# A routed expert layer: six experts in the order of their row counts, with graded capacities and shorter halves

## The chip, the cores and the metric

The kernel runs on one core of a Trainium2 chip. The metric is the device time of one execution in microseconds (us). Its engines work beside each other: TensorE (PE) multiplies matrices, with a separate row for its weight loads (PEld); VectorE (DVE) and ScalarE (ACT) work on elements; GpSimd (POOL) does elementwise work too and issues the indirect transfers; SyncE (SP) issues the plain transfers (DMA).

## The reference

The last of three stages is the one that changes. Before it, attention runs with 16 clusters over 2 batches of 768 tokens, 8 heads of 64, and then a dense feed-forward layer with 2048 hidden columns. Its output, 1536 tokens of 512 numbers, goes into a layer with eight experts; each token is computed by two of them:

```python
def _moe2_ref(x, w_gate, w_noise, noise, w1, w2):
    N, D = x.shape
    E = w_gate.shape[1]
    logits = x @ w_gate
    noise_scale = np.log1p(np.exp(x @ w_noise))
    noisy_logits = logits + noise_scale * noise
    top2 = np.argpartition(-noisy_logits, 2, axis=1)[:, :2]
    ...
    for e in range(E):
        for k in range(2):
            mask = top2[:, k] == e
            ...
            h = np.maximum(x[mask] @ w1[e], 0.0)
            out[mask] += top2_w[mask, k, None] * (h @ w2[e])
```

N is 1536, D is 512, E is 8, and `w1[e]` is 512 x 1024. So 3072 rows are computed in all, and how many an expert gets is known only once the gate has run on the chip.

## The kernel before, in words

All large matmuls are done in a split float form: each operand is kept as a high part and a remainder, and one product takes three matmuls (high by high, high by remainder, remainder by high).

The gate's result gives each token and each of its two experts a slot. `route_scatter` writes the token's row of 516 numbers (512 values and 4 of weights and indices) into a DRAM tensor `xs`, in which each expert has a region of its own; POOL issues one indirect transfer for 128 rows (L965). `route_end` (L972 to 977) then knows how many rows each expert has, and `table` (L979 to 995) writes a small table to DRAM (`tab`, L987) and computes `nr`, the number of passes over the experts. One pass is enough where no expert overflows its capacity; `rest` (L1343 on) loops over further passes and needs `nr` in a register of each engine (L1345).

Each expert is computed for a fixed number of rows, its capacity; slots behind the last real row are computed and thrown away. Experts 0 and 1 have 512 slots in two halves of HALF = 256 rows, one per batch. Their first halves (batch 0) are begun inside `middle`, beside the end of the dense layer, by a list of due times. Their second halves come in `moe2` (L1310 to 1341): `gather_half` (L1055 to 1060) fetches `Xh`, 128 partitions of 2 rows, once the scatters have landed. Experts 2 to 7 follow in the order of their numbers, each with CAP = 432 rows, 108 partitions by 4 (L1334 to 1341).

For each of these `load` fetches weights and rows. `weights` (L1040 to 1046) issues eight transfers of 512 KB in a fixed order into three staging buffers (`stg`, L1008 and L1010); ACT makes the high part (L1017) and DVE or POOL the remainder (L1021). This runs about one expert ahead of its use. `gather` (L1048 to 1052) fetches the rows `X` from the expert's region of `xs` into the one buffer "R". `turn` transposes `X` on TensorE (L1121), in tiles of 128 by 108, into `xT`, which ACT and DVE split (L1123, L1124), and computes the tokens' weights and indices from the last four columns (L1070 to 1075). After `turn` the buffer "R" is free for the next gather.

`expert` (L1275 to 1308) is the work proper. The first layer (L1217) keeps a piece of the weights stationary and moves all rows of `xT` as columns, 432 at a time: 8 blocks of hidden columns by 4 blocks of inputs by 3, 96 matmuls. ACT makes the relu (L1225), DVE the remainder (L1226). The second layer has two forms. For experts 2 to 6 (`flip`, `ffn2_t`, L1270) the rows are again the moving columns, 8 by 4 by 3 = 96 matmuls of 432 columns, and the result is transposed back (L1308). For the last expert and for the halves (`ffn2`, L1240) a block of rows is stationary and 512 columns of weights move: one set of 24 matmuls per block, four blocks of 108 rows for the last expert. `combine` scales each block by the token's weight (L1252, or L1254 where it is added to what another expert left) and POOL writes it to the output by an indirect transfer (L1255); `gather_out` (L1100, L1102) fetches beforehand what is there.

The order in which an engine gets its instructions comes from the program's order and a scheduler that ranks ready work; in `middle`, and on TensorE at the end of the last expert, it is written by hand.

Of the kernel before, what the change touches and what calls it, by code (L numbers as in the profile page):

```python
# [8 lines left out]
F32 = mybir.dt.float32  # L9
F32R = mybir.dt.float32r  # L10
# [11 lines left out]
NB = S // 128  # L22
# [5 lines left out]
E = 8  # L28
# [4 lines left out]
CK = CAP // CP  # L33
HALF = 256
MAIN = 2 * HALF
BASE = MAIN - CAP
ROUNDS = -(-NT // CAP)
REG = BASE + ROUNDS * CAP
ROW = DM + 4
# [562 lines left out]
class Moe:  # L602
# [39 lines left out]
    def init_piece(self, i):  # L642
        nc = self.nc
        n = E * CK
        if i < n:
            e, k = divmod(i, CK)
            cp = CP if e > 1 else 128
# [324 lines left out]
    def route_end(self):  # L972
        v, end = self.nc.vector, self.rtot[:, NB, 0:2]
        over = self.rtile("over", 2)
        v.tensor_scalar(over, end, float(-MAIN), 0.0, op0=OP.add, op1=OP.max)
        v.scalar_tensor_tensor(end, over, float(MAIN), self.over[:, 0], op0=OP.add, op1=OP.add)
        self.table(self.rtot[:, NB, :])

    def table(self, total):  # L979
# [3 lines left out]
        for r in range(ROUNDS):  # L983
            v.tensor_scalar_add(tb[:, r, :, 0], total, float(-BASE - r * CAP))
            v.tensor_scalar(tb[:, r, :, 1], self.ie, float(REG), float(BASE + r * CAP), op0=OP.mult, op1=OP.add)
            v.tensor_copy(tb[:, r, :, 2], self.ie)
        nc.sync.dma_start(self.tab.rearrange("(o r) n -> o (r n)", o=1), tb[0:1].rearrange("p r e n -> p (r e n)"))  # L987
        mx = self.const.tile([128, 1 + ROUNDS], F32, name="mx")
        v.tensor_reduce(mx[:, 0:1], total, axis=AX.X, op=OP.max)
        v.memset(mx[:, 1:2], 1.0)  # L990
        for r in range(1, ROUNDS):
            v.tensor_single_scalar(mx[:, r + 1:r + 2], mx[:, 0:1], float(BASE + r * CAP), op=OP.is_gt)
        self.nr = self.const.tile([128, 1], I32, name="nr")
# [45 lines left out]

    def weights(self, e, par=None):  # L1040
        fixed = par is None
        we = [w[e] if fixed else w[bass.ds(e, 1)].rearrange("o k n -> (o k) n") for w in (self.w1, self.w2)]
        W = [None] * 8
        for s in ORDER:
            W[s] = self.weights_part(e, e % 2 if fixed else par, s, we)
        return [x for p in W for x in p]

    def gather(self, e):  # L1048
        X = self.rows.tile([CP, CK, ROW], F32, tag="R", name="X")
        o = e * REG + BASE  # L1050
        self.nc.sync.dma_start(X, self.xs[o:o + CAP].rearrange("(p k) n -> p k n", k=CK))
        return X

    def gather_half(self, b):

        X = (self.rows if b else self.yp).tile([128, 2, 2, ROW], F32, tag="R" if b else "Y", name="Xh")
        for e in range(2):
# [20 lines left out]
    def gather_rest(self, e, r):  # L1078
# [6 lines left out]
                       allow_small_or_imprecise_dtypes=True)  # L1085
        v.tensor_scalar(sl[:, :, 1:2], sl[:, :, 0:1], t[:, 0:1], OOB, op0=OP.is_lt, op1=OP.mult)
        v.scalar_tensor_tensor(ix, sl[:, :, 0:1], t[:, 1:2], sl[:, :, 1:2], op0=OP.add, op1=OP.add)
# [4 lines left out]
        X = self.rows.tile([CP, CK, ROW], F32, tag="R", name="X")  # L1092
        nc.sync.dma_start(X, self.xs[bass.ds(e * REG + r * CAP + BASE, CAP)].rearrange("(p k) n -> p k n", k=CK))
        return X, self.meta(X[:, :, DM:], t[:, 2:3])
# [16 lines left out]

    def xtile(self):
        return self.xg.tile([128, KB, 2, CAP], F32R, tag="xT", name="xT")

# [11 lines left out]
    def middle(self, acc, W0, xT0, m0, we):  # L1126
# [53 lines left out]
        for fb in range(FB2):  # L1180
# [3 lines left out]
            def g(fb=fb):  # L1184
                if fb == 0:
                    ps.extend(self.bank((k,), [128, DM]) for k in (5, 6))
                self.ffn2(W0, ps, t["H", fb], fb)
# [125 lines left out]
    def moe2(self, W0, W1, xT1, m1):  # L1313
# [6 lines left out]

        self.expert(W1, xT1, m1, True, 128, second)
        self.expert(W0, nxt[0][1], nxt[0][2], False, 128, lambda: self.xpose(*nxt[1][:2], (6, 7)))

        def load(e):
            n["W"] = self.weights(e)
            n["X"] = self.gather(e)

        def turn(e):
            n["xT"] = self.xtile()
            self.xpose(n["X"], n["xT"], (6, 7))  # L1330
            n["m"] = self.meta(n["X"][:, :, DM:], float(e))

        load(2)
        done = lambda: None  # L1334
        self.expert(W1, nxt[1][1], nxt[1][2], True, 128, lambda: turn(2))
# [125 lines left out]
```

## Time and profile before

| | us |
|---|---|
| median of 3 runs | 966.37 |
| lowest, highest | 964.11, 972.53 |
| the profiled execution | 959.64 |
| its span, first to last instruction | 957.9 |

The profiled execution is 6.7 us below the median of the three runs; durations are taken from it. A busy time is an engine's own work and leaves out waits. A timeline row groups instructions that follow each other: its first number is the start of the first of them in us, its second the time to the modelled end of the last; ends of matmuls overlap the next one's start, so prices of matmuls are taken from start to start. The mean granted TensorE clock was 0.977 of 2.4 GHz.

### The profile page before, as it was taken

What the parts mean: (1) busy time and instruction counts of PE and PEld (TensorE: products, weight loads), DVE (VectorE), ACT (ScalarE), POOL (GpSimd) and SP (SyncE); (2) the same over time, 40 slices, a digit from 0 to 9 for tenths busy, and PEclk for the clock granted to TensorE, in tenths of its full rate; (3) what the DMA queues carried; (4) which work ended last, traced back from release to release, by engine and by line L of the source; (5) the groups of instructions that cost most, each with busy time, mean ns of one, the idle gap of its engine ahead of it and who ended that gap; (6) DMA issues with size and microseconds to landing.
All of it is one profiled execution on the core that took longest, in us unless ns stands there. A gap on an engine that the chain in (4) does not pass through costs nothing. (4 is left out here: it accounts for less than half of the span.)

```text
span 957.9 us, 14851 instructions
## 1 busy us (share of the span) xinstructions
PE 901.3 (94%) x5305; PEld 818.6 (85%) x5305; DVE 603.1 (63%) x1175; ACT 493.6 (52%) x1021; POOL 360.5 (38%) x400
## 2 busy tenths in 40 slices
PE   6999999999895999999999999999999999999993
PEld 3898989898784988889998989889899999999982
DVE  3889998999875677775447554826555554543321
ACT  2788888888875556554445434415434343341210
POOL 3134443445528777660000501552342433323121
PEclk8899999999998999999999998999999999999997
DMA  8756675676304433402010420464764555542011
GB/s 210 188 146 181 161 206 142 174 199 182 118 19 138 128 104 121 132 11 72 30 44 23 163 81 23 132 232 163 247 178 154 150 171 152 169 124 68 27 43 36
DMA packets 77680, 120.73 MB, mean 126 GB/s; under 512 B 9777, under 2 KB 55858, under 8 KB 76954
## 3 DMA queue, kind: packets, MB, share of 16 engines
q1 hardware_dynamic: 70114, 101.57, 36.8%
q0 software_dynamic: 7488, 18.16, 5.9%
q8 instruction: 43, 0.70, 0.3%
q14 instruction: 35, 0.29, 0.1%
HBM read 73.70 MB, written 24.36 MB: 102 GB/s over the span
## 5 line engine op out<-in xcount | busy, mean ns | idle before, releaser
L422 DVE TENSOR_TENSOR PTl<-ps_pt,PTh 128x384 fp32r<-128x384 f32 x192 | 98.4, 548 | 10.1 <-ACT PTh L417 9.2
L417 ACT ACTIVATE PTh<-ps_pt 128x384 fp32r<-128x384 f32 x192 | 87.5, 495 | 28.0 <-PE ps_pt L407 26.7
L390 DVE TENSOR_REDUCE nm<-ps_s 128x1 f32<-128x768 f32 x96 | 91.1, 948 | 12.6 <-PE ps_s L385 12.1
L729 PE MATMUL bank<-xh,wih 128*128 128x384 f32 x256 | 88.3, 345 | 10.0 <-ACT wih L713 5.0
L729 PE MATMUL bank<-xh,wil 128*128 128x384 f32 x256 | 88.3, 345 | 6.3 <-POOL wil L714 6.3
L407 PE MATMUL ps_pt<-ident,P 128*128 128x128 f32 x576 | 88.0, 276 | 4.0 <-DVE PTl L422 3.5
L398 ACT ACTIVATE P<-ps_s,nm 128x768 f32<-128x768 f32 x96 | 87.4, 910 | 5.3 <-DVE nm L390 5.3
L1217 PE MATMUL bank<-xT,wB 128*128 128x432 f32 (+1 forms) x480 | 87.1, 329 | 0.0
L729 PE MATMUL bank<-xl,wih 128*128 128x384 f32 x256 | 87.0, 340 | 0.0
L1225 ACT ACTIVATE hh<-bank 128x432 fp32r<-128x432 f32 (+1 forms) x80 | 36.8, 464 | 95.7 <-PE bank L1217 89.7
L1217 PEld LDWEIGHTS bank<-xT,wB 128*128 128x128 f32 x480 | 78.4, 188 | 4.2
L407 PEld LDWEIGHTS ps_pt<-ident,P 128*128 128x128 f32 x576 | 67.8, 141 | 15.1 <-DVE PTl L422 11.9
L1226 DVE SCALAR_TENSOR_TENSOR hl<-bank,hh 128x432 fp32r<-128x432 f32 (+1 forms) x80 | 42.0, 528 | 59.5 <-ACT hh L1225 59.2
L744 PE MATMUL bank<-woh,gh 128*128 128x512 f32 x192 | 76.2, 397 | 0.6 <-DVE Xn L484 0.6
L1021 POOL TENSOR_TENSOR wA<-stg,wA 128x512 fp32r<-128x512 f32 x16 | 20.7, 1292 | 146.8 <-DVE wol L714 69.7
L744 PE MATMUL bank<-wol,gh 128*128 128x512 f32 x192 | 75.4, 393 | 0.0
L744 PE MATMUL bank<-woh,gl 128*128 128x512 f32 x192 | 71.5, 394 | 0.0
L384 PE MATMUL ps_s<-k,q 128*128 128x384 f32 x192 | 70.2, 366 | 0.2 <-ACT P L398 0.2
L385 PE MATMUL ps_s<-k,q 80*128 80x384 f32 x192 | 66.4, 346 | 3.9 <-DMA q<-ohT 3.9
L1255 POOL DMA_INDIRECT out_dram<-Y,idx x32 | 35.7, 1117 | 74.3 <-DVE Y L1254 66.5
L729 PEld LDWEIGHTS bank<-xh,wih 128*128 128x128 f32 x256 | 49.0, 191 | 12.7 <-ACT wih L713 5.4
L1017 ACT ACTIVATE wA<-stg 128x512 fp32r<-128x512 f32 x52 | 32.4, 632 | 49.4 <-DMA stg<-in_moe_w_dram 22.4
(280 smaller groups left out, 2251.1 us busy)
## 6 DMA issues: line engine op xcount, KB each, us to landing
stg<-in_moe_w_dram SPq DMA_DIRECT2D x64, 512.0 KB
q<-ABq SPq DMA_DIRECT2D x48, 192.0 KB
k<-ABk SPq DMA_DIRECT2D x48, 192.0 KB
si<-in_moe_w_in_dram SPq DMA_DIRECT2D x14, 512.0 KB
so<-in_moe_w_out_dram SPq DMA_DIRECT2D x14, 512.0 KB
xs<-zrow SPq DMA_DIRECT2D x24, 217.7 KB
X<-xs SPq DMA_DIRECT2D x6, 870.8 KB
ld<-in_k_dram SPq DMA_DIRECT2D x8, 384.0 KB
```

Of the source, the lines that this page charges most:

```text
L384: self.nc.tensor.matmul(o, self.g("S1", u, "q")[:, h, qs], self.g("S1", u, "k")[:, h, ks], start=True, stop=False)
L385: self.nc.tensor.matmul(o, self.g("S2", u, "q")[:80, h, qs], self.g("S2", u, "k")[:80, h, ks], start=False, stop=True)
L390: self.nc.vector.tensor_reduce(nm, self.g("s", j)[:, :, :384], axis=AX.XY, op=OP.max, negate=True)
L398: self.nc.scalar.activation(P, self.t.pop(("s", j))[:, :, :384], AF.Exp, bias=self.t.pop(("nm", j)), scale=1.0, accum_out=self.g("sums", u ...
L407: self.nc.tensor.transpose(ps[:, k, :], P[:, k * 128:(k + 1) * 128], self.ident)
L417: self.nc.scalar.activation(self.pt_at(j, g, 0), self.g("pt", j, g), AF.Copy)
L422: self.nc.vector.tensor_sub(self.pt_at(j, g, 1), self.t.pop(("pt", j, g)), f(self.pt_at(j, g, 0)))
L729: nc.tensor.matmul(h, w[:, kb, :], x[b][:, kb, sl], start=(kb == 0 and x is self.xh and w is wih), stop=(kb == KB - 1 and w is wil))
L744: nc.tensor.matmul(acc[j], g[:, sl], w, start=(fb == 0 and n == 0), stop=(fb == FB1 - 1 and n == 2))
L1217: self.nc.tensor.matmul(ps, w[:, kb, :], xT[:, kb, x], start=(kb == 0 and i == 0), stop=(kb == KB - 1 and i == 2))
L1225: self.nc.scalar.activation(hh, ps, AF.Relu)
L1226: self.nc.vector.scalar_tensor_tensor(hl, ps, 0.0, f(hh), op0=OP.max, op1=OP.subtract)
```

## The change

- HALF falls from 256 to 240, held as 120 partitions by 2 rows.
- Experts 2 to 7 run in the order of their row counts, largest first. The place in that order sets the capacity: 432, 416, 408, 400, 392 and 384. The last place is three blocks of 128 rows, the others four blocks of 108, 104, 102, 100 and 98.
- The order is found on DVE in a new function `rank` between `route_end` and `table`. SP reads each place's expert number into a register, and the addresses of the weights and of `X` are computed from it. `turn` compares with the expert number out of a tile.
- `table` and the overflow passes take account of the graded capacities, with three rounds in place of four.

```diff
-HALF = 256
+HALF = 240
+CH = HALF // 2
...
+CAPS = ((108, 4), (104, 4), (102, 4), (100, 4), (98, 4), (128, 3))
+CMIN = min(cp * ck for cp, ck in CAPS)
...
+        self.rank(self.rtot[:, NB, :])
         self.table(self.rtot[:, NB, :])
+    def rank(self, total):
+        c, v, n = self.const, self.nc.vector, E - 2
...
+        v.scalar_tensor_tensor(key, total[:, 2:], float(E), self.ie[:, 2:], op0=OP.mult, op1=OP.subtract)
...
+        v.tensor_tensor(big, row(key), col(key), op=OP.is_gt)
+        v.tensor_reduce(pos.rearrange("p (n o) -> p n o", o=1), big, axis=AX.X, op=OP.add)
+        v.tensor_tensor(big, row(pos), col(self.ie[:, :n]), op=OP.is_equal)
...
+        v.tensor_copy(self.ordi, self.ord)
...
-    def weights(self, e, par=None):
-        fixed = par is None
-        we = [w[e] if fixed else w[bass.ds(e, 1)].rearrange("o k n -> (o k) n") for w in (self.w1, self.w2)]
+    def weights(self, e, par):
+        we = [w[bass.ds(e, 1)].rearrange("o k n -> (o k) n") for w in (self.w1, self.w2)]
...
-    def gather(self, e):
-        X = self.rows.tile([CP, CK, ROW], F32, tag="R", name="X")
-        o = e * REG + BASE
-        self.nc.sync.dma_start(X, self.xs[o:o + CAP].rearrange("(p k) n -> p k n", k=CK))
+    def gather(self, e, cp, ck):
+        X = self.rows.tile([cp, ck, ROW], F32, tag="R", name="X")
+        self.nc.sync.dma_start(X, self.xs[bass.ds(e * REG + BASE, cp * ck)].rearrange("(p k) n -> p k n", k=ck))
...
         def load(e):
-            n["W"] = self.weights(e)
-            n["X"] = self.gather(e)
+            i = self.nc.values_load(self.ordi[0:1, e - 2:e - 1], engines=(mybir.EngineType.SP,), min_val=2, max_val=E - 1)
+            n["W"] = self.weights(i, e % 2)
+            n["X"] = self.gather(i, *CAPS[e - 2])
...
         def turn(e):
-            n["xT"] = self.xtile()
+            cp, ck = CAPS[e - 2]
+            n["xT"] = self.xtile(cp * ck)
...
-            done = self.expert(W, xT, m, True, CP, lambda: turn(e + 1) if e + 1 < E else None, done, e == E - 1,
+            done = self.expert(W, xT, m, True, CAPS[e - 2][0], lambda: turn(e + 1) if e + 1 < E else None, done, e == E - 1,
                                e < E - 1)
```

TensorE gets 24 matmuls fewer in all, those of the fourth block of the last expert. Instructions that wait for a register, and what the scheduler ranks behind them, stand elsewhere on SP and on TensorE. First SP, while the first halves end: the first weight load of the first of the six experts (`stg_8029` before), the table, and what goes before the gather `X`. Before:

```order
L1008 DMA stg_8029<-in_moe_w_dram 128x4x256
L987 DMA tab<-tb 1x128
L1345 TENSOR_LOAD nr
L1345 ISA x2
L1010 DMA stg_8037<-in_moe_w_dram 128x2x512
L1008 DMA stg_8047<-in_moe_w_dram 128x4x256
L1059 DMA Xh<-xs 128x1032 x2
L1010 DMA stg_8055<-in_moe_w_dram 128x2x512
L1008 DMA stg_8065<-in_moe_w_dram 128x4x256
L1051 DMA X<-xs 108x2064
```

With the change, the same place up to the table (`stg_8064` is the first weight load of the first of the six):

```order
L1045 DMA stg_7590<-in_moe_w_dram 128x2x512
L1359 TENSOR_LOAD ordi
L1359 ISA x2
L1043 ISA
L1043 DMA stg_8064<-in_moe_w_dram 128x4x256
L1359 TENSOR_LOAD ordi
L1359 ISA x2
L1019 DMA tab<-tb 1x128
L1359 TENSOR_LOAD ordi
```

The first weight load now stands behind a register load of `ordi`, the order, and four more register loads follow the rows shown before `nr` is read. Further down on SP the gather `X` came behind five of that expert's weight loads before (the last row of the first piece); now it comes behind all eight:

```order
L1043 DMA stg_8100<-in_moe_w_dram 128x4x256
L1045 ISA
L1045 DMA stg_8110<-in_moe_w_dram 128x2x512
L1043 ISA
L1043 DMA stg_8120<-in_moe_w_dram 128x4x256
L1045 ISA
L1045 DMA stg_8130<-in_moe_w_dram 128x2x512
L1084 ISA
L1084 DMA X<-xs 108x2064
L1043 ISA
```

What moved there is the gather: the three weight loads that followed it now go ahead of it. Last, TensorE, where the transposes of `X` for the first of the six experts begin. `xT_7763` and `xT_7797` are the transposed rows of experts 0's and 1's second halves in the two programs, `hh` a relu result. Before, they begin in the second half of expert 0:

```order
L1217 MATMUL bank_7948<-xT_7763,wA_6296 128x256
L1121 MATMUL bank_8297<-ident,X 128x108 x4
L1121 MATMUL bank_8304<-ident,X 128x108
L1240 MATMUL bank_7814<-wA_6872,hh_7938 128x512
L1240 MATMUL bank_7814<-wA_6873,hh_7938 128x512
L1240 MATMUL bank_7815<-wA_6872,hh_7938 128x512
L1240 MATMUL bank_7815<-wA_6873,hh_7938 128x512
L1121 MATMUL bank_8304<-ident,X 128x108 x2
L1217 MATMUL bank_7965<-xT_7763,wA_6299 128x256 x2
L1217 MATMUL bank_7965<-xT_7763,wA_6300 128x256
L1217 MATMUL bank_7965<-xT_7763,wA_6299 128x256 x2
```

With the change:

```order
L1251 MATMUL bank_8161<-xT_7797,wB_7185 128x240
L1251 MATMUL bank_8161<-xT_7797,wB_7184 128x240 x2
L1251 MATMUL bank_8161<-xT_7797,wB_7185 128x240
L1155 MATMUL bank_8332<-ident,X 128x108 x4
L1155 MATMUL bank_8339<-ident,X 128x108
L1251 MATMUL bank_8192<-xT_7797,wB_7358 128x240 x2
L1251 MATMUL bank_8192<-xT_7797,wB_7359 128x240
L1251 MATMUL bank_8192<-xT_7797,wB_7358 128x240 x2
L1251 MATMUL bank_8192<-xT_7797,wB_7359 128x240
L1251 MATMUL bank_8192<-xT_7797,wB_7358 128x240 x2
L1251 MATMUL bank_8192<-xT_7797,wB_7359 128x240
L1274 MATMUL bank_8142<-wB_7207,hh_8157 120x512
```

The transposes moved from the second half of expert 0 into that of expert 1, behind the second group of its first layer's matmuls; the matmuls around them are 240 columns wide in place of 256.

## Rows read from the trace of the kernel before

**Rows 1.** The page: busy us (share of the span) and instructions of TensorE.
```profile
PE 901.3 (94%) x5305; PEld 818.6 (85%) x5305; DVE 603.1 (63%) x1175; ACT 493.6 (52%) x1021; POOL 360.5 (38%) x400
```

**Rows 2.** Windows: us; busy of PE, PEld, DVE, ACT, POOL (instructions); PEclk; DMA share; GB/s.
```profile
734.60:775.43 40.83, 40.83 (x224) 38.86 (x223) 22.36 (x36) 14.73 (x30) 15.63 (x12) 1.00 0.49 152
775.43:816.43 41.00, 41.00 (x225) 38.99 (x224) 22.51 (x40) 16.99 (x33) 14.50 (x12) 1.00 0.57 167
816.43:857.76 41.33, 41.32 (x225) 39.04 (x224) 20.20 (x37) 14.79 (x29) 14.22 (x12) 1.00 0.47 144
857.76:898.86 41.10, 41.10 (x226) 38.96 (x225) 14.69 (x27) 8.86 (x18) 9.63 (x9) 1.00 0.21 62
898.86:941.70 42.84, 42.84 (x209) 35.83 (x207) 12.58 (x18) 4.46 (x9) 11.19 (x11) 1.00 0.16 49
941.70:957.90 16.20, 0.15 (x1) 0.00 (x0) 0.75 (x1) 0.00 (x0) 1.12 (x2) 0.57 0.09 27
```

**Rows 3.** Waits of TensorE from 580 to 693 us: total, times, longest.
```profile
PE bank L1121 <- DMA Xh<-xs: 1.3, 1, 1.3
```

**Rows 4.** Timeline of TensorE: start us, us, line, tiles, shapes, count.
```profile
576.18 0.34 PE L729 MATMUL bank<-xh,wih 128*128 128x384 f32 x1
...
578.27 0.38 PE L1121 MATMUL bank<-ident,Xh 128*128 128x128 f32 x2
...
650.77 1.58 PE L1217 MATMUL bank<-xT,wg 128*128 128x256 f32 x12
652.19 1.09 PE L1240 MATMUL bank<-wA,hh 128*128 128x512 f32 x4
653.12 0.62 PE L1240 MATMUL bank<-wA,hl 128*128 128x512 f32 x2
...
788.98 2.53 PE L1217 MATMUL bank<-xT,wA 128*128 128x432 f32 x12
791.35 0.56 PE L1270 MATMUL bank<-hh,wA 128*128 128x432 f32 x2
...
814.88 0.91 PE L1121 MATMUL bank<-ident,X 108*128 108x108 f32 x8
815.56 0.45 PE L1270 MATMUL bank<-hl,wA 128*128 128x432 f32 x1
```

**Rows 5.** Waits of SP's queue from 605 to 700 us.
```profile
SPq L1059 <- DMA xs<-R,rridx: 6.1, 2, 5.6
```

**Rows 6.** Timeline of SP, 605 to 700 us: weight loads and gathers.
```profile
618.06 0.37 SPq L1008 DMA_DIRECT2D stg<-in_moe_w_dram  x1
...
630.95 0.39 SPq L1010 DMA_DIRECT2D stg<-in_moe_w_dram  x1
...
638.94 0.83 SPq L1059 DMA_DIRECT2D Xh<-xs  x2
...
655.64 1.49 SPq L1051 DMA_DIRECT2D X<-xs  x1
...
663.20 0.37 SPq L1010 DMA_DIRECT2D stg<-in_moe_w_dram  x1
...
682.11 0.33 SPq L1051 DMA_DIRECT2D X<-xs  x1
...
689.23 0.37 SPq L1010 DMA_DIRECT2D stg<-in_moe_w_dram  x1
```

**Rows 7.** Timeline of DVE, where the row counts are done.
```profile
619.15 0.16 DVE L976 SCALAR_TENSOR_TENSOR rtot<-rover,over 128x2 f32<-128x2 f32 x1
```

**Rows 8.** Line L1345, register load of nr on SP: ns min/median/max.
```profile
L1345 SPq TENSOR_LOAD <-nr x1: 702/702/702, 621.9 to 621.9; - x1
```

**Rows 9.** Timeline of TensorE, transposes of X for experts 2 and 3.
```profile
663.74 0.65 PE L1121 MATMUL bank<-ident,X 108*128 108x108 f32 x5
...
672.98 0.54 PE L1121 MATMUL bank<-ident,X 108*128 108x108 f32 x4
...
688.36 0.66 PE L1121 MATMUL bank<-ident,X 108*128 108x108 f32 x5 [0.35 <-DMA X<-xs]
```

More of the change, by code (lines that the diff above doesn't have):

```diff
@@ L982, in table @@
         v.memset(tb, 0.0)
-        for r in range(ROUNDS):
-            v.tensor_scalar_add(tb[:, r, :, 0], total, float(-BASE - r * CAP))
-            v.tensor_scalar(tb[:, r, :, 1], self.ie, float(REG), float(BASE + r * CAP), op0=OP.mult, op1=OP.add)
+        for r in range(1, ROUNDS):
+            o = BASE + CMIN + (r - 1) * CAP
+            v.tensor_scalar_add(tb[:, r, :, 0], total, float(-o))
+            v.tensor_scalar(tb[:, r, :, 1], self.ie, float(REG), float(o), op0=OP.mult, op1=OP.add)
             v.tensor_copy(tb[:, r, :, 2], self.ie)
+        v.tensor_scalar_add(tb[:, 1, :, 3], self.cap, float(-CMIN))
         nc.sync.dma_start(self.tab.rearrange("(o r) n -> o (r n)", o=1), tb[0:1].rearrange("p r e n -> p (r e n)"))
         mx = self.const.tile([128, 1 + ROUNDS], F32, name="mx")
-        v.tensor_reduce(mx[:, 0:1], total, axis=AX.X, op=OP.max)
+        left = self.const.tile([128, E], F32, name="left")
+        v.scalar_tensor_tensor(left, self.cap, float(BASE), total, op0=OP.add, op1=OP.is_lt)
+        v.tensor_mul(left, left, total)
+        v.tensor_reduce(mx[:, 0:1], left, axis=AX.X, op=OP.max)
         v.memset(mx[:, 1:2], 1.0)
         for r in range(1, ROUNDS):
-            v.tensor_single_scalar(mx[:, r + 1:r + 2], mx[:, 0:1], float(BASE + r * CAP), op=OP.is_gt)
+            v.tensor_single_scalar(mx[:, r + 1:r + 2], mx[:, 0:1], float(BASE + CMIN + (r - 1) * CAP), op=OP.is_gt)
         self.nr = self.const.tile([128, 1], I32, name="nr")
@@ L1110, in xpose, with xtile @@
             self.xpose_part(X, xT, kb, banks)
[L1112 to L1113 removed]
+    def xtile(self, n=CAP):
+        return self.xg.tile([128, KB, 2, n], F32R, tag="xT", name="xT")
     def xpose_part(self, X, xT, kb, banks):
@@ L1185, in g @@
                 if fb == 0:
-                    ps.extend(self.bank((k,), [128, DM]) for k in (5, 6))
+                    ps.extend(self.bank((k,), [CH, DM]) for k in (5, 6))
                 self.ffn2(W0, ps, t["H", fb], fb)
@@ L1319, in second @@
             self.xpose(*nxt[0][:2], (6, 7))
[L1321 to L1322 removed]
+        self.expert(W1, xT1, m1, True, CH, second)
+        self.expert(W0, nxt[0][1], nxt[0][2], False, CH, lambda: self.xpose(*nxt[1][:2], (6, 7)))
         def load(e):
[L1325 to L1326 removed]
+            i = self.nc.values_load(self.ordi[0:1, e - 2:e - 1], engines=(mybir.EngineType.SP,), min_val=2, max_val=E - 1)
+            n["W"] = self.weights(i, e % 2)
+            n["X"] = self.gather(i, *CAPS[e - 2])
         def turn(e):
[L1329 removed]
+            cp, ck = CAPS[e - 2]
+            n["xT"] = self.xtile(cp * ck)
             self.xpose(n["X"], n["xT"], (6, 7))
[L1331 removed]
+            n["m"] = self.meta(n["X"][:, :, DM:], self.ord[:cp, e - 2:e - 1])
         load(2)
         done = lambda: None
[L1335 removed]
+        self.expert(W1, nxt[1][1], nxt[1][2], True, CH, lambda: turn(2))
         for e in range(2, E):
```

31 lines of the change are left out of this document (24 added, 7 removed).

## The prediction

> **What bounds the kernel now.** I read the page first: TensorE is busy for 94% of the span and no other engine comes near [rows 1], so the first guess is that only matmul time counts. A share over the whole span proves nothing about one stage, so the second view is the table of windows, cut at the last layer's experts. From expert 3 on every window is TensorE from end to end: 40.83 of 40.83 us, 41.00 of 41.00, 41.32 of 41.33, 41.10 of 41.10, and 42.84 of 42.84 for expert 7, at granted clock 1.00 (2.4 GHz), with DVE at most 22.5 us and the DMA engines at most 0.57 busy [rows 2]. So there a column less is time less, until DVE or the weights become the limit, and they have 18 us of room in each expert. Behind the last matmul lies a tail of 16.20 us that holds no expert work [rows 2]; the change doesn't touch it. Third, the waits of TensorE over the halves of experts 0 and 1: it stands 1.3 us for `Xh`, the second halves' rows [rows 3]. There a shorter matmul turns into a longer wait; the gathers of `X` for experts 2 and 3 come close to it too (below). Fourth, the price of a matmul. Durations of single matmuls overlap in the profile, so I take start to start in the timeline: 256 columns (652.19 − 650.77)/12 = 0.118 us, 384 columns, twelve of them before the next kind, (578.27 − 576.18)/12 = 0.174, 432 columns (791.35 − 788.98)/12 = 0.1975, 512 columns (653.12 − 652.19)/4 = 0.2325 [rows 4]. From 256 to 432 that is 0.45 ns a column; from 432 to 512 it is 0.44, from 384 to 432 it is 0.49. I take 0.45 and keep 0.44 and 0.49 as ends.
>
> **The change part by part.**
>
> Capacities of experts 3 to 6. Each of these runs 96 first-layer matmuls (8 blocks, 4 x 3) and 96 second-layer ones with the rows as moving columns, 192 together. The second to fifth place lose 16, 24, 32 and 40 columns: 192 x 0.45 ns x (16 + 24 + 32 + 40 = 112) = 9.7 us (9.5 to 10.5). The first place keeps 432 and gains nothing.
>
> Last expert. Its 96 first-layer matmuls lose 48 columns: 96 x 48 x 0.45 ns = 2.1 us (the 384-column row itself gives 96 x 23 ns = 2.2). Its second layer moves 512 columns once per block of rows, so the columns stay and the blocks count: three of 128 rows for four of 108, 8 x 3 = 24 matmuls fewer, 24 x 0.2325 = 5.6 us. Together 7.7. It is the largest piece for a single expert, and the only one that takes instructions away.
>
> Transposes. The smaller `X` tiles save 4 to 10 columns in 16 transposes an expert, and the last has 12 for 16; at 85 ns for 108 columns [rows 4] all of them give about 0.3 us.
>
> Halves. 384 matmuls go from 256 to 240 columns. By the slope each saves 7 ns. Half of them lie ahead of `Xh`. `Xh` is issued at 638.94, when the scatters have landed, for which SP waited 5.6 us [rows 5, 6], and TensorE already stands for it [rows 3]; the scatters run on POOL and don't depend on how wide a matmul is. So what the first halves save, 192 x 7 ns = 1.4 us, comes back as a longer wait for `Xh`: I cost it at 0 (0 to 1.4). The second halves have no such wait: 192 x 7 ns = 1.4 us. The trace has no split-float matmul under 256 columns, so this price is an estimate. From below: if 240 columns take what 256 take, 0. From above: the slope. Far on the other side stands the first rival. I take the slope, because the points from 256 to 512 lie on it.
> The Trainium skill ("TensorE: Matmul & The Clock Gate", section "Back-to-back issue gap") gives columns/2.4 + 2.5 ns for one matmul behind another, alone: 182.5 for 432 columns, where the row says 197.5. By its slope of 0.417 ns the sum below would be 18.0 us instead of 19.1; I stay with the rows' slope.
>
> Ranking. Sixteen or so small DVE instructions now follow L976, at 619.15; one like them takes 0.16 us [rows 7]: about 2.5 us. Behind them on DVE stand the last relu remainders of the first halves and the `Y` of L1252; on SP, the `tab` store, the loads of the six order registers and expert 2's first weight load. TensorE has its work from tiles made before, so I cost the DVE part at 0, with 2.5 us if that cover is gone. SP's part: seven register loads at 0.70 us each [rows 8], 4.9 us from about 622; if the checks behind each take half as much again, 7.4, they end near 629. Expert 2's first weight load moves with them from 618.06 to about 622.5. The next weight load went out at 630.95 [rows 6], when a buffer came free, so SP is in time: 0; uncovered, at most 7.4.
>
> Dynamic addresses. Every weight load and `X` gather gets a register instruction on SP, which has idle time between loads. 0.
>
> Order on SP. The scheduler now issues each `X` behind all eight weight loads of its expert. For expert 2 that moves the gather from 655.64 to behind the load at 663.20, for expert 3 from 682.11 to behind 689.23 [rows 6]. `X` of expert 3 was first used at 688.36 after a wait, so it takes 688.36 − 682.11 = 6.3 us to land [rows 9]. Then expert 2's lands near 663.7 + 6.3 = 670.0. TensorE first used it at 663.74, but in the new order its first transposes stand behind the second group of expert 1's second half, where the old run reached 672.98 [rows 9]; less 1.4 us for the shorter halves and 0.7 for eight transposes that are no longer ahead of it, 670.9. So it is just in time, with some 0.9 us of slack, and expert 3's is alike, landing at 696. I cost both at 0 (0 to 5 us slower). From expert 4 on the gather waits for the old `X` to be transposed, and has some 25 us.
>
> Sum: 9.7 + 7.7 + 0.3 + 1.4 = 19.1 us. The profiled execution took 959.64 us (span 957.9 and 1.7 around it), so 940.5 there. It is 6.7 us under the median of 966.37; the same amount off the median gives 947.3, and I forecast 947. Ends: 17.1 us saved (slope 0.44, nothing from halves or transposes) to 22 (slope 0.49, both halves). The three runs spread from 964.11 to 972.53; with that the likeliest case reaches from 940 to 954.
>
> **The rivals.**
>
> A, slower: 240-column matmuls fall out of the rate. Of split-float matmuls every width in the trace is 256 or more, and nothing shows that the line goes on below. The longest float rows below it, the transposes, cost 85/108 = 0.79 ns a column [rows 4]; at that rate 240 columns take 189 ns, 71 more than 256 took, and all 384 are on TensorE's path: + 27 us, against 17.7 saved elsewhere: 9.6 us slower, 976. If the rate fell to four times the slope, 432 ns, it would be + 121 us, 1069. It decides from the point where 384 matmuls lose 17.7 us, 46 ns each, that is 164 ns for 240 columns. For it: the kernel's widths all stop at 256. Against it: 256 itself is on the line, and the transposes, narrower still, show no fourfold cost.
>
> B: the gathers come late. If the stage buffers come free 2 to 4 us later than now (POOL and DVE convert them among other work), `X` of experts 2 and 3 lands behind its use, and TensorE stands about 2.5 us at each: 5 us back, 952. For it: 0.9 us of slack. Against it: the loads ahead of it no longer share the DMA engines with `X`.
>
> C: the change doesn't do what it says, because one expert has more rows than its place allows. The overflow loop would then run: eight experts of at least 41 us each [rows 2], + 330 us, 1280. For it: six counts, in falling order, must stay within 432, 416, 408, 400, 392 and 384, with an average near 384 (3072 rows over eight experts). Against it: the reference's own inputs, drawn with its seed 0, give experts 2 to 7 the counts 409, 396, 390, 374, 374 and 369, and halves of 186 to 195 rows; each fits.
>
> **How the numbers follow.** Likeliest 0.68, B 0.12, A 0.18, C 0.02. About 1% is what a measurement of this kernel tells from no change, 9.7 us. The likeliest case and B save 12 us or more; I leave 0.05 of their 0.80 for losses that add up to less than 1% gained. So faster has 0.75; the same takes that 0.05 and 0.03 of A's cheap end, 0.08; slower has the rest of A and C, 0.17. The range starts at 939, below the likeliest case's 940, and reaches to 968, over B and over a partial A; what is left out is most of A and C.
>
> **What would show it.** In the profile after, windows of experts 3 to 6 should be near 39.4, 38.9, 38.6 and 37.6 us, each filled by TensorE, and the last near 35.1; start to start should be 0.190, 0.187, 0.183, 0.179 and 0.174 us for 416 down to 384 columns, and 0.111 for 240. The wait for `Xh` should grow by about 1.4 us from 1.3. If 240 columns stand at 0.16 us or more, A holds; if TensorE waits for `X` by more than 1 us, B; a second pass over the experts is C. The forecast is wrong if a window of experts 3 to 6 is shorter in columns and not in time.

## The result, and the profile after

The changed kernel took 953.8 us (median of 4 runs, 952.65 to 955.92), the kernel before 969.45 us beside it (4 runs, 964.11 to 972.55): a ratio of 0.9896, 95% interval 0.9847 to 0.9944. The forecast was 947 us, a ratio of 0.980. The direction is right, but by this ratio about half of the forecast saving is missing. The ratio is not the quotient of these two medians, which is 0.984 and just below its interval, so the first comparison is a rough one. Three later comparisons of the same two kernels gave 0.9851 (0.9809 to 0.9892), 0.9863 (0.9827 to 0.9900) and 0.9844 (0.9811 to 0.9877), that is 13.5, 13.6 and 15.4 us between medians where 19.1 were forecast: there a fifth to three tenths of the saving is missing.

The page of the changed kernel has TensorE's share a little lower than [rows 1], and its busy time 14.4 us less, with 28 instructions fewer, as many as the 24 matmuls and four transposes that the last expert loses:

```profile
PE 886.9 (93%) x5277; PEld 813.9 (85%) x5277; DVE 598.8 (63%) x1190; ACT 491.8 (52%) x1021; POOL 359.3 (38%) x398
```

The windows, cut at the first matmul of each of the six experts (first place to last), answer to [rows 2]; the columns are us, busy time and instructions of PE, PEld, DVE, ACT and POOL, granted clock, DMA share, GB/s:

```profile
699.64:741.57 41.93, 40.76 (x216) 38.41 (x214) 21.16 (x36) 17.50 (x35) 13.43 (x11) 1.00 0.58 163
741.57:787.20 45.63, 42.30 (x225) 41.11 (x224) 20.34 (x36) 14.46 (x30) 14.08 (x12) 0.93 0.54 147
787.20:827.84 40.64, 39.35 (x225) 38.39 (x225) 21.63 (x39) 16.41 (x32) 14.70 (x12) 1.00 0.55 164
827.84:865.93 38.09, 38.09 (x225) 37.72 (x225) 20.25 (x36) 14.60 (x30) 14.56 (x12) 1.00 0.57 173
865.93:903.23 37.30, 37.30 (x222) 36.98 (x221) 14.30 (x28) 8.29 (x17) 9.88 (x9) 1.00 0.22 64
903.23:938.60 35.37, 35.37 (x187) 31.83 (x185) 10.95 (x18) 4.32 (x9) 8.82 (x9) 1.00 0.17 51
...
754.60:761.40 6.80, 5.54 (x16) 5.24 (x17) 5.07 (x9) 3.51 (x7) 2.22 (x2) 0.50 0.49 161
```

The last three experts are where the forecast had them: 38.1, 37.3 and 35.4 us for 38.6, 37.6 and 35.1. The third place misses by 1.7 us (40.64 for 38.9), and the second is far off: 45.63 us where 39.4 were forecast, longer than any expert before, with a mean clock of 0.93. That is the sign which the prediction named last, a window shorter in columns and not in time. The last row shows where that comes from: for 6.80 us the granted clock was 0.50, the lower of the two levels (1.2 GHz). The waits of TensorE say what stood ahead of it:

```profile
PE bank L1274 <- ACT hh L1259: 5.7, 1, 5.7
PE bank L1304 <- ACT hh L1259: 4.4, 2, 3.3
PE bank L919 <- DVE rrM L869: 2.4, 1, 2.4
PE bank L1155 <- DMA X<-xs: 2.1, 2, 1.2
```

The wait for the second halves' `Xh` [rows 3] isn't among them. New are a wait of 5.7 us near 628 us, in the first halves, and 4.4 us for relu results inside the experts, which in the profile of before was this row:

```profile
PE bank L1270 <- ACT hh L1225: 0.7, 1, 0.7
```

The prediction named neither.

**The wait in the second place**, followed back. On TensorE (start, us, line, tiles, shapes, count):

```profile
752.10 0.43 PE L1251 MATMUL bank<-xT,wB 128*128 128x416 f32 x1
755.86 3.14 PE L1304 MATMUL bank<-hh,wB 128*128 128x416 f32 x8 [3.33 <-ACT hh L1259]
```

On ACT, in the order in which it ran them:

```profile
746.36 0.52 ACT L1259 ACTIVATE hh<-bank 128x416 fp32r<-128x416 f32 x1 [3.83 <-PE bank L1251]
754.25 1.15 ACT L1052 ACTIVATE wB<-stg 128x512 fp32r<-128x512 f32 x2 [7.37 <-DMA stg<-in_moe_w_dram]
755.31 0.50 ACT L1259 ACTIVATE hh<-bank 128x416 fp32r<-128x416 f32 x1
```

The relu (L1259 at 755.31) that TensorE needs stands behind a weight conversion (L1052) of an expert that runs two places later, and that conversion waits 7.37 us for its transfer. On SP's queue, the transfers:

```profile
727.77 0.37 SPq L1045 DMA_DIRECT2D stg<-in_moe_w_dram  x1
741.35 0.29 SPq L1084 DMA_DIRECT2D X<-xs  x1
741.90 0.37 SPq L1043 DMA_DIRECT2D stg<-in_moe_w_dram  x1
742.51 0.37 SPq L1045 DMA_DIRECT2D stg<-in_moe_w_dram  x1
743.93 0.37 SPq L1043 DMA_DIRECT2D stg<-in_moe_w_dram  x1
```

SP issued nothing from 728 to 741.35. Its waits name the reason, the gather of `X`, whose buffer the transposes had not yet released:

```profile
SPq L1084 <- PE bank L1155: 13.0, 1, 13.0
```

Three weight loads stood behind it and went out within 2.6 us of it: two at once, the third after 0.8 us more for its own buffer. In the kernel before, at the same point, the first two had gone out ahead of the gather:

```profile
729.59 0.37 SPq L1008 DMA_DIRECT2D stg<-in_moe_w_dram  x1
730.90 0.37 SPq L1010 DMA_DIRECT2D stg<-in_moe_w_dram  x1
734.57 0.33 SPq L1051 DMA_DIRECT2D X<-xs  x1
```

**The terms of columns** hold. Start to start in the changed kernel's timeline:

```profile
661.07 1.51 PE L1251 MATMUL bank<-xT,wA 128*128 128x240 f32 x12
662.42 0.37 PE L1155 MATMUL bank<-ident,Xh 120*128 120x120 f32 x2
...
765.40 2.44 PE L1251 MATMUL bank<-xT,wB 128*128 128x416 f32 x12
767.67 0.25 PE L1155 MATMUL bank<-ident,X 102*128 102x102 f32 x1
```

(662.42 − 661.07)/12 = 0.112 us for 240 columns (forecast 0.111) and (767.67 − 765.40)/12 = 0.189 for 416 (forecast 0.190). A step in the price below 256 columns, rival A, is not there.

### The profile page after: what moved, and what is told of

Read it like the earlier page. It is cut to its first block, busy times and chain, and to the rows that moved or that the text cites. A ratio compares the mean times of both kernels' runs of the same rounds, so it can differ in the third digit from the quotient of the medians.

```text
span 954.2 us, 14930 instructions
## 1 busy us (share of the span) xinstructions
PE 886.9 (93%) x5277; PEld 813.9 (85%) x5277; DVE 598.8 (63%) x1190; ACT 491.8 (52%) x1021; POOL 359.3 (38%) x398
## 5 line engine op out<-in xcount | busy, mean ns | idle before, releaser
L1259 ACT ACTIVATE hh<-bank 128x240 fp32r<-128x240 f32 (+6 forms) x80 | 35.2, 446 | 99.8 <-PE bank L1251 83.5
L1251 PE MATMUL bank<-xT,wB 128*128 128x240 f32 (+3 forms) x480 | 83.0, 321 | 0.0
L1260 DVE SCALAR_TENSOR_TENSOR hl<-bank,hh 128x240 fp32r<-128x240 f32 (+6 forms) x80 | 40.3, 506 | 57.5 <-ACT hh L1259 56.8
L1289 POOL DMA_INDIRECT out_dram<-Y,idx x31 | 33.0, 1066 | 78.3 <-DVE Y L1288 68.5
L733 PEld LDWEIGHTS bank<-xh,wil 128*128 128x128 f32 x256 | 49.2, 192 | 9.6 <-POOL wil L718 9.5
```

The source lines that it names most:

```text
L733: nc.tensor.matmul(h, w[:, kb, :], x[b][:, kb, sl], start=(kb == 0 and x is self.xh and w is wih), stop=(kb == KB - 1 and w is wil))
L1251: self.nc.tensor.matmul(ps, w[:, kb, :], xT[:, kb, x], start=(kb == 0 and i == 0), stop=(kb == KB - 1 and i == 2))
L1259: self.nc.scalar.activation(hh, ps, AF.Relu)
L1260: self.nc.vector.scalar_tensor_tensor(hl, ps, 0.0, f(hh), op0=OP.max, op1=OP.subtract)
```

## The experiments

My theory after this reading had two parts: the six register loads in a row hold other engines back and make the stall near 628 us, and the gathers' new place on SP makes the waits in the experts. Eighteen runs went into it. Runs under one heading below share a chip, and the kernel before was timed beside them each time. "Stretch" below means the time from the first second-layer matmul of the six experts to the last matmul of all; "the part before it" begins at the last routing matmul.

**Four kernels for the two parts.** The first writes the order into the program (6, 7, 3, 2, 5, 4), which also gives SP's queue its old order:

```diff
+SEQ = (6, 7, 3, 2, 5, 4)
...
-            i = self.nc.values_load(self.ordi[0:1, e - 2:e - 1], engines=(mybir.EngineType.SP,), min_val=2, max_val=E - 1)
+            i = SEQ[e - 2]
...
```

> Same capacities and halves as the change, but the order of the experts is written into the program (6, 7, 3, 2, 5, 4): no ranking, no register loads, fixed addresses, and SP's queue gets its old order back. Theory (register loads in a row and the gathers' place on SP together cost what is missing): TensorE's waits from 611 us to the end fall from some 13 us to 3 or less, and the kernel takes about 942 us against 954 for the change. Rival (the shorter matmuls themselves expose waits for ACT, DVE or weights): the waits for relu results stay at 8 us or more in all, and it takes 950 or more.

955.26 us (951.66 to 959.72), ratio 0.9884 (0.9853 to 0.9915). The theory's 942 is missed. The wait in the second place is gone, the stall near 628 us is not (5.7 us), without a single register load of the order. Against the change's second profile on this chip (below) the stretch is 3.7 us shorter (226.2 for 229.9), but the part before it 2.6 us longer (98.0 for 95.4), and the last routing matmul itself came 4.0 us later (613.5 for 609.6 us). Why it came later, in a part that the edit doesn't aim at, is open, so this run is no clean measure of the old order.

The second puts six unused register loads into the kernel before:

```diff
...
         def load(e):
+            self.nc.values_load(self.ordi[0:1, e - 2:e - 1], engines=(mybir.EngineType.SP,), min_val=2, max_val=E - 1)
             n["W"] = self.weights(e)
```

> The kernel before with six unused register loads on SP, in the place where the change has them; nothing else. Theory (the register loads hold back the semaphores of ACT and DVE while they run): ACT's relu of the first halves stands several us, TensorE waits 4 to 6 us for it, and the kernel is 4 to 8 us slower than before. Rival (the ranking on DVE delays the relu remainders): no wait, within 1 us of before.

967.38 us, ratio 1.0011 (0.9986 to 1.0036). The stall was in this profile (5.5 us), as the theory wanted, and yet the time is that of before. So either its cause isn't the loads, or before has it too.

The third reads all six numbers by one register load, and the fourth gives the gathers their old places:

```diff
+        _, ids = self.nc.values_load_multi_w_load_instructions(self.ordi[0:1, :], engines=(mybir.EngineType.SP,), min_val=2, max_val=E - 1)
```

> The change with one register load that reads all six expert numbers at once. Theory (the loads in a row): the 5.7 us wait of TensorE near 628 us falls under 1.5 us, with the low clock behind it, and the time falls by 5 to 8 us to 946 to 949. Rival (dynamic addresses or ranking make the stall): it stays at 952 or more, with the wait still above 4 us.

952.43 us, ratio 0.9856 (0.9831 to 0.9882), and the stall stays at 5.8 us:

```profile
PE bank L1274 <- ACT hh L1259: 6.2, 2, 5.8
```

With the static order, which has none of these loads, and the kernel before with six, this says that register loads are not its cause: the first part of the theory fell.

```diff
+                if j == 4 and e < 4:
+                    n["X"] = self.gather(ids[e - 2], *CAPS[e - 2])
...
+            if e >= 4:
+                if e + 1 < E:
+                    stage(e + 1, ORDER[:2])
+                n["X"] = self.gather(ids[e - 2], *CAPS[e - 2])
```

> The change with each gather of X issued where it stood before: behind five of its expert's weight loads for the first two, behind two of the next expert's for the others. Register loads stay six in a row. Theory (the gather that waits for the buffer holds back weight loads behind it): TensorE's waits for relu results in experts 3 to 6, 4.4 us in the change, fall under 1 us, and the time falls by 4 to 6 us to about 949, while the 5.7 us wait near 628 us stays. Rival (loads with register addresses are slower in themselves): waits of 3 us or more stay in the experts and the time stays above 952.

952.46 us, ratio 0.9856 (0.9832 to 0.9880). The wait in the second place and its low clock are gone; waits for `X` of 2.1 us and smaller ones for relu results and remainders stand in other places, and the time is that of the kernel with one register load, which has the wait. The theory's 949 is missed. Beside that kernel the stretch is 5.3 us shorter (226.1 for 231.4) and the part before it 2.3 us longer (98.5 for 96.2).

**Is the stall the change's?** The kernel before was profiled again, beside the change.

> The kernel before, unchanged, profiled a second time. Theory (the stall of ACT and TensorE while the scatters run belongs to both kernels, and the profiled execution of before, 6.7 us under its median, is one that was spared it): TensorE stands 5 to 6 us for a relu result near 628 us, and the run takes 963 to 970 us. Rival (the stall comes with the change, by its register loads, ranking or narrower halves): no such wait and a run of 958 to 961 us.

It has the stall. Its waits of TensorE, and ACT's rows at the place (the second row's wait ended with a semaphore for which the profile names no sender):

```profile
PE bank L1240 <- ACT hh L1225: 5.4, 1, 5.4
...
PE bank L1121 <- DMA X<-xs: 0.6, 2, 0.4
```

```profile
619.42 0.38 ACT L1225 ACTIVATE hh<-bank 128x256 fp32r<-128x256 f32 x1 [0.33 <-issue]
629.99 0.66 ACT L1225 ACTIVATE hh<-bank 128x256 fp32r<-128x256 f32 x2 [10.19 <-remote]
```

964.21 us. So the stall belongs to both kernels. The profiled execution that the prediction was worked out from was spared it; the profile of the change was not. From the last routing matmul to the last of all it took 332.2 us, this one 338.3; so the stall may be why it lay 6.7 us under its median, but that is not shown: a later profile without the stall (`base_third`, on another chip) lies at its median. The two first profiles can't be laid side by side around 628 us, and their difference of 3.7 us is no measure of the change.

> The change, unchanged, timed beside the others on one chip. Theory (the gather ahead of weight loads costs some 5 us in experts 3 to 6): 953 to 956 us, with 4 us or more of waits for relu results behind 700 us, and the stretch from the first second-layer matmul of the six experts to the end takes 247 us as in its first profile. Rival (that loss was chance of one execution): the waits are gone in this profile and the stretch takes 243 us or less.

951.50 us, ratio 0.9851 (0.9809 to 0.9892): 3.5 us of wait in the second place, as in the first profile.

**Both edits, and the halves.** Beside them ran the kernel with one register load and all gathers in their old places:

> One register load for all six experts and the gathers in their old places, together. Theory (only the gathers matter; the register loads don't): within 1 us of the kernel with the gathers alone, 952, and 3 to 5 us faster than the change on this chip; stretch of the six experts 242 us. Rival (both parts cost): 2 us or more under the gathers alone, 950 or less.

948.33 us, ratio 0.9816 (0.9780 to 0.9853): 3.2 us under the change. And the change with `HALF = 256`:

> The change with halves of 256 rows again. By the slope its second halves lose 1.4 us; by the theory that the first halves only wait longer, nothing there: 1 to 2 us slower than the change on this chip. Rival (narrower halves bring the stall forward or make it): 3 us or more faster than the change, without the 5.7 us wait.

952.63 us, 1.1 us over the change, but its runs spread from 944.47 to 957.86, so this says only that the halves are worth little. In its profile the wait in the second place is 5.5 us, 2.0 more than in the change's, which alone could make the difference. The stall is there too (5.2 us), so narrow halves don't make it.

**Parts alone.** On another chip, three kernels: the kernel before with register loads and addresses and nothing else, so that SP's queue has the order of the change; the combined kernel with POOL's scatters in groups of four; the kernel before with halves of 240 rows:

```diff
...
+            i = self.nc.values_load(self.ordi[0:1, e - 2:e - 1], engines=(mybir.EngineType.SP,), min_val=2, max_val=E - 1)
+            n["W"] = self.weights(i, e % 2)
+            n["X"] = self.gather(i)
```

> The kernel before, with capacities and halves as they were and the experts in their old order, but with the expert numbers read into registers, so that SP's queue takes the order of the change (each gather of X behind all eight weight loads of its expert, ahead of the next expert's). Theory (the gather that waits for its buffer holds back weight loads): TensorE waits 3 us or more for relu results inside experts 2 to 6, the stretch from their first second-layer matmul to the last matmul of all grows from 241 us to 244 or more, and the kernel is 3 to 6 us slower than before. Rival (the late loads only bite where experts are shorter, 39 us in place of 41): stretch 242 or less and no difference.

960.64 us, ratio 1.0001 (0.9969 to 1.0032). The stretch grew to 244.3 us, as the theory had it, by one wait of 2.1 us and low clock behind it; the time didn't, as the rival had it. Beside a profile of the kernel before on this chip (`base_third`) the stretch is 3.4 us longer and the part before it 3.9 us shorter (90.9 for 94.8). So the order as a whole costs nothing here, but that isn't the same as late weight loads costing nothing.

```diff
...
+            nc.gpsimd.tensor_copy(rx, self.ridx[:, j])
...
```

> The kernel with one register load and the gathers in their old places, and with POOL's ten scatters in a row broken into groups of four, each behind a small copy of its indices and with weight remainders between. Theory (a long run of scatters on POOL holds back the semaphores of other engines until it ends): the 5.8 us wait of TensorE for the relu result near 628 us falls under 2 us; what the later scatters add to the wait for Xh may take 2 to 6 us of it back, so 942 to 950 us. Rival (the stall has another cause, such as code loading or the register loads): the wait stays above 4 us and the time is 948 or more.

957.44 us, ratio 0.9946 (0.9914 to 0.9979). The stall is absent, but it is absent too from the two kernels beside it, which have the scatters in one row, so the run tells nothing of its cause. Its wait for `Xh` is 6.3 us, where the last scatter starts at 641.1 us (631.8 in `both_again`, with a wait of 3.6).

> The kernel before with halves of 240 rows, nothing else. Prediction's term: the second halves save 192 x 7 ns = 1.4 us, the first halves nothing as they wait longer for Xh: the stretch from the last routing matmul to the first second-layer matmul of expert 2 falls from 97.5 to about 96 us, and the kernel is 1 to 2 us faster. Rival (both halves count): 2.8 us faster, stretch near 94.7.

962.67 us, ratio 1.0023 (0.9996 to 1.0050): nothing saved. In its profile TensorE's work is 1.7 us less than in `base_third` (table below) and its gaps are 0.5 us more: 2.1 us for `Xh` in place of 1.5, 1.6 for `X` in place of 3.0, and 1.2 for relu results. That would leave 1.2 us; where the time lost it is not shown.

**The same on a chip without the stall.** Before, change, and the two kernels with the gathers moved, once more:

> The kernel before, unchanged, profiled beside the three that follow on one chip, as their base for stretches. If the stall near 628 us is a matter of the execution or the chip and not of the kernel, it stands here exactly where it stands in the three others; the stretch of the six experts up to the last matmul takes 240 to 242 us either way.

963.79 us, no stall:

```profile
PE bank L1121 <- DMA X<-xs: 3.0, 2, 2.3
PE bank L915 <- DVE rrM L865: 2.3, 1, 2.3
PE bank L1121 <- DMA Xh<-xs: 1.5, 1, 1.5
```

> The change, unchanged. Theory (gathers ahead of weight loads cost 5 to 6 us of the forecast 17.7 in the experts, on every chip and in every execution): waits for relu results of 3 us or more behind 700 us, stretch 230 to 231.5 us, time 8 to 13 us under before. Rival (those waits came with the stall, whose delay of the conversions they are): without the stall they are under 1 us and the stretch is 227 or less.

949.38 us, ratio 0.9863 (0.9827 to 0.9900). The wait in the experts stands here too, so it doesn't come from the stall:

```profile
PE bank L1304 <- ACT hh L1259: 4.8, 2, 3.7
PE bank L1155 <- DMA Xh<-xs: 2.6, 1, 2.6
...
PE bank L1155 <- DMA X<-xs: 1.5, 2, 0.8
```

> The change with each gather of X in its old place on SP, register loads single. Theory: stretch 226 us, waits for relu results under 1.5 us, 3 to 5 us faster than the change on this chip. Rival: stretch and time as the change's, within 1 us.

949.78 us, ratio 0.9865 (0.9821 to 0.9909). The stretch is the theory's 226 us and the time the rival's: the part before it is 5.2 us longer than in the change's profile beside it, with 3.8 us of wait for `Xh` and 2.8 for `X`.

> As the one before with a single register load. Theory (register loads cost nothing that TensorE waits for): within 1.5 us of the kernel with six loads, stretch 224 to 226 us, 3 us or more faster than the change. Rival (the loads on SP delay expert 2's first weights): 2 us or more under the kernel with six loads.

950.85 us, ratio 0.9884 (0.9834 to 0.9933): within 1.1 us of six loads. The register loads cost nothing that can be seen here, but the stretch was 231 us where the theory had 224 to 226, with waits of 2.1 and 1.3 us in later experts. Moving all gathers takes the wait away, and other waits stand in its place.

**One gather.** What was left was to move only the gather that the wait hangs on, that of the third place. These runs share a third chip:

```diff
...
+            if e in (4,):
+                stage(e + 1, ORDER[:2])
+            n["X"] = self.gather(ids[e - 2], *CAPS[e - 2])
```

`stage` issues the loads of a weight piece and leaves its conversion to later.

> The change, unchanged, as the base of the two that follow on this chip. Theory: the wait for a relu result near 750 us (3.3 to 3.7 us in three profiles) is here again, with 6.8 us of half clock behind it; 12 us under before. Rival: without it the change is 6 us faster than in the other profiles.

950.94 us, ratio 0.9844 (0.9811 to 0.9877), with 3.9 us of wait in the second place.

> The change with one gather moved: the X of the expert in third place goes out behind two weight loads of the next expert; the gathers of the first two and of the others stay where the change has them. Theory (that one gather, waiting for its buffer, holds back the weight loads which the relu near 750 us stands behind): the wait near 750 us falls under 0.5 us, the half clock behind it goes, and the kernel is 5 to 7 us faster than the change on this chip. Rival (the loss moves to the next late load, as with all gathers moved): idle time and half clock in sum as in the change within 2 us, and the time too.

944.94 us (944.05 to 946.90), ratio 0.9787 (0.9760 to 0.9815): 6.0 us under the change on the same chip, and the fastest of all. Its windows (columns as above), SP's queue and its waits:

```profile
736.02:775.48 39.46, 39.46 (x225) 38.80 (x224) 19.24 (x36) 14.48 (x30) 15.58 (x12) 1.00 0.50 153
775.48:816.05 40.57, 39.44 (x225) 38.48 (x225) 21.49 (x39) 16.41 (x32) 14.68 (x12) 1.00 0.55 165
```

```profile
730.90 0.37 SPq L1043 DMA_DIRECT2D stg<-in_moe_w_dram  x1
733.92 0.37 SPq L1045 DMA_DIRECT2D stg<-in_moe_w_dram  x1
735.79 0.29 SPq L1084 DMA_DIRECT2D X<-xs  x1
```

```profile
PE bank L1274 <- ACT hh L1259: 5.7, 1, 5.7
...
PE bank L1155 <- DMA X<-xs: 0.9, 1, 0.9
PE bank L1304 <- ACT hh L1259: 0.8, 1, 0.8
```

The second place takes 39.46 us, the forecast's number, at full clock; the third still takes 40.6 for 38.9, as in the change, with waits of 0.8 us for a relu and 0.3 for a remainder in it. The two weight loads go out at 730.90 and 733.92, ahead of the gather, as in the kernel before.

> As the one before, with the gathers for the fourth and fifth places also behind two weight loads of the next expert. Theory: besides the wait near 750 us the smaller one near 815 us (1.1 us) goes: 1 to 2 us faster than with one gather moved. Rival (two buffers held by early loads make the other experts' weights late): new waits of 1 us or more near 810 to 850 us, and no gain over one gather.

946.39 us, ratio 0.9796 (0.9768 to 0.9823): no better than one gather, with waits of 1.5 and 1.1 us near 814 and 846 us, as the rival had it.

**The account.** From the last routing matmul to the last matmul of all, in us: TensorE's gaps over 0.1 us, summed from its timeline; half the length of the times at clock 0.50, gaps in them left out; and the rest, which is matmul work at full clock. Rows of one chip stand together. Two profiles of the same matmuls differ by up to 0.8 us in work (327.8 for `base_third`, 327.0 for `e_bdyn`).

| kernel, profile | whole | gaps | low clock | work |
|---|---|---|---|---|
| before, second | 338.3 | 6.0 | 4.3 | 328.0 |
| change, second | 325.3 | 10.2 | 6.7 | 308.4 |
| before, third | 335.7 | 4.5 | 3.4 | 327.8 |
| change, third | 323.1 | 8.9 | 6.4 | 307.8 |
| before, halves of 240 | 334.5 | 5.0 | 3.4 | 326.1 |
| change, fourth | 326.9 | 11.8 | 7.5 | 307.6 |
| one gather moved | 320.4 | 8.2 | 4.2 | 308.0 |

Cut at the first second-layer matmul of the six experts, the profiles suggest what the place of the first two gathers does. With halves of 240 rows and the stall, the part before the cut took 95.4 to 96.3 us in the six profiles that have them where the change has them, and 98.0 to 98.5 us in the three that have them in their old places (`e_static`, `e_gather`, `e_both`). Without the stall it is 92.0 us for the change and 97.2 and 95.2 with all gathers moved. The first profile of the kernel before, 90.2 us with the old places and no stall, doesn't fit, so this is no proof. The stretch behind the cut is 224.8 us with one gather moved, 223.8 to 226.2 with all in their old places and the stall (226.2 and 231.4 without it), and 229.9 to 231.4 in the change and the kernel with one register load.

## Why the prediction was wrong where it was

**The work** was forecast right. It fell by 19.6 and 20.0 us; the forecast was 19.1, and beside it at most 1.4 for the first halves. The columns' slope, the last expert's 24 matmuls (its window is 35.4 us for 35.1) and the price of 240 columns hold. Rival A is out, and so is C, whose second pass would have added some 330 us.

**The step that failed** is "Order on SP", where the prediction wrote "I cost both at 0 (0 to 5 us slower). From expert 4 on the gather waits for the old `X` to be transposed, and has some 25 us." It asked when the gathered rows would be needed, and there the answer was about right: waits for `X` came to 2.1, 0.8, 1.5 and 1.9 us in the four profiles of the change, for 0.3, 0.6 and 3.0 in three of the kernel before. Rival B's sign, more than 1 us, is there in profiles of both kernels; its 5 us are not. It didn't ask what stands behind a gather that waits. For the third place these are weight loads, two of them with free buffers, then the conversions on ACT that wait for them, then the relu behind the conversions, then TensorE: 13.0 us of waiting on SP became 3.3 us on TensorE. That wait is 3.3 to 3.9 us in four profiles of the change. The 18 us of room that the prediction gave the weights in each expert are a mean over a window (DMA engines 0.54 busy in the one that failed); a load that isn't issued has no use of it.

**The price of this wait was nearly twice its length.** From 754.60, inside the wait, the granted clock was 0.50 for 6.80 us; TensorE was busy for 5.54 of them, which at full clock would have taken half, 2.8 us less. A wait of 1.1 us for a relu at 821 us in the same profile had no low clock behind it. In the account gaps grew by 4.2 and 4.4 us and low clock by 2.4 and 3.0, together 6.6 and 7.4 us, which is what lies between the work saved and the stretch. The Trainium skill ("TensorE: Matmul & The Clock Gate", section "HAM oscillation — how this bites in real kernels") says that a TensorE which waits for transfers between bursts begins the next burst throttled, and counts half of the throttled time as the penalty; the 3.33 us wait and the 6.80 us row at 0.50 agree with it, though here TensorE waited for ACT, which waited for the transfer. The prediction gave waits their length alone, in rival B as well.

**Shown, and how far.** That the wait comes from the gather's place is shown by moving that one gather: wait and low clock go, 6.0 us come back, and the ratio is 0.9787 where 0.980 was forecast. The saving there is 21.4 us between medians for 19.1 forecast, which doesn't prove every term: the sum left out the first halves, and the tail behind the last matmul, about 0.6 us shorter in the profiles of the changed kernels (15.4 for 16.0 in the first two), where the prediction wrote that the change doesn't touch it. With experts of 41 us the same order lengthened the stretch by 3.4 us (one wait of 2.1 us) and the time by nothing. Moving every gather gave less: 3.2 us under the change on one chip, nothing on another, though there with a wider spread. From the part before the experts, the likely reason is that the change's places for the first two gathers are better than the old ones by 2 to 5 us, which the prediction, with 0 to 5 us slower, didn't consider. That is read from the profiles; the first two gathers were not moved alone.

**Halves.** The term of 1.4 us for the second halves didn't show as time: alone, the narrower halves gave 1.0023 (0.9996 to 1.0050), which leaves 0.4 us at most. As work it is plausible but not measured apart: the 1.7 us above are for the 312 narrower matmuls behind the last routing matmul, of both halves, for which the slope gives 2.2, and two profiles of one work differ by 0.8. What took the saving back is open; the wait for `X`, which could have, was not longer than in `base_third`. In the change the wait for `Xh` grew from 1.5 to 2.6 us on one chip, about as forecast.

**Ranking, register loads and addresses** cost nothing that TensorE waits for, as forecast: six loads in a row in the kernel before gave 1.0011 (0.9986 to 1.0036), and one load in place of six made no difference beyond the spread (1.1 us more on one chip). The loads took longer than forecast, 10.8 us in the first profile (624.0 to 634.8, with the stall) for 4.9 to 7.4, and 7.2 us in the third, without it; the weight load behind them went out at 635.28 in the first for 630.95 before. TensorE stood for neither.

**The base.** The sum was made against an execution without the stall near 628 us and then taken off the median; how many of the unprofiled runs have the stall isn't known. This did little harm, since the stall is in both kernels; it would have misled a comparison of the two first profiles.

## What to carry to other kernels

Where a change moves an instruction that waits on a queue, price what is queued behind it and who waits for that, not only when its own result is needed; here a gather with some 25 us to spare, by the prediction's estimate, held back weight loads that had none. The same order of a queue can cost in one stage and save in another, so try each moved instruction alone. A wait of several us on TensorE is counted with the low clock behind it, which here cost nearly as much again. Profile the kernel before twice: an execution several us under its median may lack something that others have.

## What was not expected of the hardware

In the first halves, while POOL issues ten scatters one after the other, ACT stands some 10 us for a semaphore in many profiles: 10.19 us in the row above, with 5.4 us of wait on TensorE. On one chip it stood in all eight profiles taken, on a second in all three, on a third in none of seven, whatever the kernel: the change, the kernel before, static order, register loads or none. The first profile of the change has it too. In all twelve profiles that have it ACT went on 1.8 to 2.1 us after the tenth scatter had ended, also where the scatters ran some 4 us later (`e_static`). That the scatters hold it back is a guess from this; the run with the scatters in groups fell on the chip without the stall, and what decides is open.
